# Two runs of four mixer chunks per batch instead of three runs, and the half tile moved to the last chunk

## The chip, the cores and the metric

The kernel runs on one core of a Trainium2 chip. TensorE (PE) multiplies matrices into PSUM banks, VectorE (DVE) and ScalarE (ACT) read those banks and work on SBUF, GpSimd (POOL) and SyncE (SP) issue DMAs. The metric is the device time of one launch in microseconds (us); smaller is better. Times quoted with a place, such as "358.13", are us from the first instruction of the profiled execution.

## The reference

Eight batches (B = 8) of a gated attention unit are followed by a low-rank token mixer. For each batch, with S = 3136 tokens, D = 256 channels and 64 query channels:

```
scores = (z @ z.T) / S            # S x S, z is S x 64
attn   = max(scores, 0) ** 2
x      = u * (attn @ v)           # S x 256, the attention's output
h      = (x.T @ U @ V).T          # U: S x 32, V: 32 x S
y      = x + h
out    = y + max(y @ w_ch1, 0) @ w_ch2     # 256 -> 1024 -> 256
```

The kernel multiplies in bf16 and accumulates in float32.

## The kernel before

**Tiles and turns.** The 3136 tokens are 24 tiles of 128 and one of 64 (tile 24, called NF in the code, the half tile). A batch is 25 *turns*; turn i makes the attention output of tile (12 + i) mod 25, so the half tile is turn 12. One turn is about 50 matmuls of line 471 (`half`), each with 64 contraction rows: two of them, on the upper and lower half of the array, run at the same time. The half tile's products (line 511, `quarter`) use quarters of the array, 64 by 64. Two turns share a pair of PSUM banks, of which there are two sets; `open_pair` takes the other set for each new pair of turns, and `close_pair` adds the two banks (ACT copy L485, DVE add L486), multiplies by u (L501) and leaves x in the SBUF pool `x_bf`. For the half tile two ACT copies (L497) and a DVE add (L498) stand between L486 and L501. The half tile is a pair of its own, turns 13 and 14 are the next pair.

**Scores.** `score` (L358) computes blocks of z zT two at a time into one of two PSUM buffers of the ring `ps2`; ACT applies max(.,0) (L371) and DVE squares (L373) into the panels A. Only half of the symmetric score matrix is computed; the other blocks come from DMA transposes of a panel into a *strip* (`turn`, L393, issued by SP). The strips are issued six turns ahead and there are seven strip buffers. Score steps of this batch stand in turns 0 to 9, those of the next batch in turns 14 to 24; turns 10 to 13 have none.

**The mixer of the batch before.** While batch b is attended, batch b-1 is mixed. After turn 0, `rank_sums` (L566) and `rank_close` (L578, L580) make t1 = x.T @ U. In seven of the turns `low_rank` (L621) computes V.T @ t1 for one *chunk* of three or four tiles into the PSUM set that is not being accumulated (`spare()`), two DVE instructions (L635) add it to x, and a DMA transpose (`turn_x`, L594) makes ut, the transposed chunk; there are three ut buffers. Where the next pair of turns begins, it opens that same set and waits for the two L635. A *burst* n is the four *up* steps of chunk n (L653: four matmuls each into a `ps2` buffer, then a relu on ACT, L671) merged with the *down* steps of chunk n-1 (L700: eight matmuls per tile into a bank of `spare()`, then a DVE add with x, L718, into one of two `o_sb` buffers, and a store, L731; the half tile needs a second DVE add, L726). Up and down use the whole 128 by 128 array; the half tile's down products use 128 by 64 halves of it. Burst 0 is special: every second up step goes to the spare set, with half the relu on DVE (L661).

Bursts stand together in *runs* behind a turn: `bursts_at` gives for each turn the bursts that follow it. In the kernel before, batch b runs bursts 6 and 7 of batch b-2 after turn 0, bursts 0 to 2 of batch b-1 after turn 6, and bursts 3 to 5 after turn 13. In the last batch, bursts 6 and 7 of batch 6 wait until attention is over (`late`), and batch 7 is mixed after that, burst by burst, with nothing beside it.

**What sets the order.** It is written out by hand: each engine takes its instructions in the order in which the Python code records them, and semaphores only make them wait. `place_groups` finds room in `x_bf` (34 tiles) from the turns at which chunks begin and end. `_merge` interleaves lists evenly, `_spread` puts score steps evenly between the 25 steps of a turn. `low_rank` is inserted into its turn at step 17, 12, 9 or 10.

The lines that matter below:

```
            if b and i in ahead:
                at = 17 if (i + (i > FIRST)) % 2 == 0 else 12 if i == 7 else 9 if i == 3 else 10
                main.insert(at, lambda c=ahead[i]: low_rank(b - 1, c))
...
            hold[0] = spare()[1 - n]          # down: bank 1 for the chunk's first pair of tiles, bank 0 for the second
```

Of the kernel before, what the change touches and what calls it, by code (L numbers as in the profile page):

```python
# [31 lines left out]
def _merge(*lists):  # L32

    keyed = [
        ((i + 0.5) / len(part), n, s)
        for n, part in enumerate(lists)
        for i, s in enumerate(part)
    ]
    return [s for _, _, s in sorted(keyed, key=lambda e: e[:2])]
# [3 lines left out]
def kernel(  # L43
# [100 lines left out]

    chunks = [[0, 1, 2, 3], [4, 5, 6, 7], [8, 9, 10, 11], [12, 13, 14]]
    chunks += [[15, 16, 17, 18], [19, 20, 21, 22], [23, 24]]
    chunks = [[turns(i) for i in c] for c in chunks]
    widths = [sum(P if t < NF else TAIL for t in c) for c in chunks]  # L150
    NC = len(chunks)
# [1 line left out]

    def bursts_at(b):

        at = {0: (NC - 1, NC)} if b > 1 else {}
        if b:
            at.update({6: (0, 1, 2), 13: (3, 4, 5)})
        if b == B - 1:
            at[17] = (NC - 1, NC)  # L160
        return at

    def place_groups():

# [512 lines left out]
    def down_steps(b, c):  # L677
        pairs = []
        for t in chunks[c]:
            if pair_of(t)[0] == t:  # L680
                pairs.append([])
            pairs[-1].append(t)
        at = {}
        for t in chunks[c]:
            at[t] = sum(P if k < NF else TAIL for k in at)
        hold = {}

        apart = b == B - 1 and c == NC - 1

        def step(n, k):  # L690
            pair = pairs[n]
            if k == 0:
                hold[0] = spare()[1 - n]
            ps = spare()[n] if apart and k else hold[0]
            q = at[pair[k]]
            for ht in range(NH):

                two = pair[k] == NF
                r = halves[ht % 2] if two else slice(0, P)
                mm(  # L700
                    out=ps[r, k * D : (k + 1) * D],
                    lhsT=relus[c][:, ht, q : q + (TAIL if two else P)],
                    rhs=w2_bf[:, ht, :],
                    start=(ht < 1 + two),
                    stop=(ht >= NH - 1 - two),
                )
            if apart or k == len(pair) - 1:
                k0 = k if apart else 0
                t, nk = pair[k0], k + 1 - k0
                if k0 == 0:  # L710
                    if c in (0, 3) and b + 2 < B:
                        hold[1] = both_pool.tile([P, 512], FP32, name="both")
                        hold[1] = hold[1].rearrange("p (t d) -> p t d", d=D)
                    else:
                        hold[1] = out_pool.tile([P, 2, D], FP32, name="o_sb")
                o_sb = hold[1][:, k0 : k + 1, :]
                p = P if t < NF else TAIL
                nc.vector.tensor_tensor(  # L718
                    out=o_sb[:p].rearrange("p t (a c) -> p t a c", c=P),
                    in0=split(ps[:p, k0 * D : (k + 1) * D]),  # L720
                    in1=x_at(b, t, nk)[:p],
                    op=ALU.add,
                )
                if t == NF:
                    o_flat = o_sb[:TAIL, 0, :]
                    nc.vector.tensor_tensor(  # L726
                        out=o_flat, in0=ps[halves[1], :D], in1=o_flat, op=ALU.add
                    )
                store = pool_dma if b + 1 < B else nc.sync.dma_start
                if t < NF:  # L730
                    store(out=rows(out[b])[:, t : t + nk, :], in_=o_sb)  # L731
                else:
                    store(out=out[b, NF * P :, :], in_=o_sb[:TAIL, 0, :])

        return [
            lambda n=n, k=k: step(n, k) for n in range(len(pairs)) for k in range(len(pairs[n]))
        ]
# [205 lines left out]
    for b in range(B):  # L943
        more = b + 1 < B
        begin = 0 if b else 2 * NG
        all_bursts.append(bursts_of(b))
        burst_at = bursts_at(b)
        v_in = list(V_PARTS) if more and b else []
        own = own_at if b else first_at
        wide = list(range(V_PARTS[3][0], NF, 2))  # L950
        wide = [(t, min(t + 2, NF)) for t in wide]
        fetch_at = dict(zip((12, 13, 14, 16, 17, 18, 20, 21), wide))
        cast_at = {i + 2: [] for i in fetch_at}
        ahead = dict(zip((2, 3, 4, 7, 10, 11, 14), range(NC)))
        for i in range(begin, NT):
            o = turns(i)
            fill = [s for key in own.get(i, ()) for s in score_steps(b, *key)]
            if b == 0 and i in first_new:
                fill += rebuild_steps(b, first_new[i])
            if b == 0 and i in first_more:  # L960
                fill.append(lambda args=first_more[i]: make_stored(*args))
            if b == 0 and i == begin:
                fill = panel + fill
            if more:
                coming = next_at if b else after_first
                fill += [s for key in coming[i] for s in score_steps(b + 1, *key)]
                if b and i == (1 if b > 1 else 5):
                    load_z(b + 1, WHOLE)
                if i == (7 if b > 1 else 11 - 2 * b):
                    turn_z(b + 1, (FIRST, NF))  # L970
                if i == (10 if b else 12):
                    turn_z(b + 1, (0, FIRST))
                if b == 0 and i == 14:
                    mirror_z((FIRST, NF))
                if i in (16, 18, 20) and v_in:
                    load_v(b + 1, v_in.pop(0))
                if b == 0 and i == 10:
                    load_v(b + 1, V_PARTS[-1])
                if b == 0 and i in cast_at:
                    (ta, tb), v_f = cast_at[i]  # L980
                    nc.gpsimd.tensor_copy(out=v_both[1][:, ta:tb, :], in_=v_f)
                if b == 0 and i == 15:
                    mirror_z((0, FIRST))
                    extend_z(b + 1)
            main = attend_steps(b, o)
            if b and i in ahead:
                at = 17 if (i + (i > FIRST)) % 2 == 0 else 12 if i == 7 else 9 if i == 3 else 10
                main.insert(at, lambda c=ahead[i]: low_rank(b - 1, c))
            _spread(main, fill)
            if b == 0 and i in first_turns:  # L990
                for t in first_turns[i]:
                    turn(b, t)
            else:
                now = b * NT + i
                for k in range(turned_to[0] + 1, min(now + lead(b, i), NT * B - 1) + 1):
                    turn(k // NT, turns(k % NT))
                    turned_to[0] = k
            if b == 0 and more and i in fetch_at:
                ta, tb = fetch_at[i]
                v_f = out_pool.tile([P, 2, D], FP32, name="o_sb")[:, : tb - ta, :]  # L1000
                nc.sync.dma_start(out=v_f, in_=rows(v[b + 1])[:, ta:tb, :])
                cast_at[i + 2] = (ta, tb), v_f
            if not more and i == NT - AHEAD:
                turn_x(b, 0)
            if b * NT + i in puts:
                puts[b * NT + i]()
            if (b, i) == ((1, 1) if more or b else (0, 20)):
                second_w()
            if b and i == 0:
                ps = spare()[0]  # L1010
                rank_sums(b - 1, ps)
                rank_close(b - 1, ps)
            for n in burst_at.get(i, ()):
                up, down = all_bursts[b - 1 if i else b - 2][n]
                if i and not more and n >= NC - 1:
                    late += up + down
                    up, down = [], []

                steps = [down.pop(0)] if n == 4 and n == burst_at[i][0] else []
                steps += _merge(up, down)  # L1020
                if more:
                    steps = _merge(steps, [lambda part=part: load_v(b + 1, part) for part in [v_in.pop(0)]])
                    if n == 3:
                        steps.insert(2, lambda: mirror_z((FIRST, NF)))
                        steps.insert(4, lambda: mirror_z((0, FIRST)))
                        steps.insert(6, lambda: extend_z(b + 1))
                run(steps)


# [49 lines left out]
```

## Time and profile before

| | |
|---|---|
| median of 3 runs | 992.9 us (992.23, 992.9, 1012.01) |
| the profiled execution's own time | 992.78 us |
| its span, first to last instruction | 991.1 us |
| TensorE busy | 981.4 us (99%) |
| ScalarE busy | 615.2 us (62%) |
| VectorE busy | 554.9 us (56%) |
| DMA transposes of strips, issue to landing, median | 5.4 us |
| stores from `o_sb` by POOL, issue to landing, median | 3.0 us |

Busy shares are averages over the whole span. Within a batch, a run begins after turn 6 at 363.81 and ends at 381.40, the half tile's turn begins at 396.54, the run behind turn 13 goes from 400.91 to 419.59. In these views, an instruction row gives its start, its duration (for a merged row, from the first start to the last end), engine, line, operation, operands and shapes, and how often it stands there; a matmul's duration contains its way through the array, so consecutive matmuls overlap, and what a matmul costs is read from start to start. The profiled program has the same lines as the kernel shown.

### The profile page before, as it was taken

How to read it: one execution, taken by the hardware profiler on the slowest of the kernel's cores; microseconds unless marked ns; L12 is line 12 of the kernel's file. 1: busy time of each engine (PE TensorE's matmuls, PEld its weight loads, DVE VectorE, ACT ScalarE, POOL GpSimd, SP SyncE). 2: the span in 40 equal slices, each digit the busy share in tenths (PEclk: the TensorE clock that was granted, in tenths of full speed). 3: DMA queues.
4: the chain of work that ended last, by engine and by line, in shares of the span. 5: the costliest groups of instructions: out<-in, count | busy, mean ns of one | idle time of the engine just before them, and what ended most of it. 6: DMA issues, size and time to landing. Idle time of an engine off the chain costs nothing.

```text
span 991.1 us, 31081 instructions
## 1 busy us (share of the span) xinstructions
PE 981.4 (99%) x13672; PEld 815.1 (82%) x13672; DVE 554.9 (56%) x1025; ACT 615.2 (62%) x845; POOL 172.9 (17%) x319
## 2 busy tenths in 40 slices
PE   8999999999999999999999999999999999999998
PEld 6788878888888888788887888878888788788876
DVE  6889834657446574375653655646546466352342
ACT  7978764757547575575745757467664676643154
POOL 5122112211121211212112121121211201111000
PEclk9999999999999999999999999999999999999999
DMA  9999979899799897898997999999889796595443
GB/s 189 167 200 229 203 155 215 149 193 184 148 177 183 165 181 144 182 180 172 169 162 168 190 162 171 164 169 187 156 166 193 156 189 135 117 201 115 81 109 100
DMA packets 400409, 165.40 MB, mean 167 GB/s; under 512 B 375617, under 2 KB 384001, under 8 KB 400273
## 3 DMA queue, kind: packets, MB, share of 16 engines
q1 hardware_dynamic: 372672, 98.11, 60.7%
q0 software_dynamic: 27600, 65.30, 27.1%
q8 instruction: 107, 1.75, 0.7%
q14 instruction: 30, 0.24, 0.1%
HBM read 61.88 MB, written 25.69 MB: 88 GB/s over the span
## 4 chain that ended last, share of the span: by engine, by line
PE 94%; DVE 3%; ACT 1%; DMA 1%; issue 0%; DVEq 0%
PE ps L471 49%; PE ps L653 17%; PE ps L700 17%; PE ps L358 7%; DVE A L373 2%; PE ps L621 1%; PE ps L511 1%; ACT A L371 1%; PE ps L566 1%; DMA strip<-A 1%; DVE both L486 0%; DMA out_dram<-o_sb 0%; PE ps L268 0%; DVE V_bf L331 0%; PE ps L284 0%
## 5 line engine op out<-in xcount | busy, mean ns | idle before, releaser
L371 ACT ACTIVATE A<-ps 128x832 bf16<-128x832 f32 (+9 forms) x481 | 358.0, 765 | 137.8 <-PE ps L358 132.5
L471 PE MATMUL ps<-v,A 64*128 64x256 bf16 x4988 | 341.2, 269 | 1.7 <-DVE A L373 1.6
L373 DVE TENSOR_TENSOR A<-A 128x832 bf16<-128x832 bf16 (+9 forms) x481 | 244.8, 527 | 130.4 <-ACT A L371 128.1
L471 PE MATMUL ps<-v,strip 64*128 64x256 bf16 x4420 | 310.1, 269 | 0.2 <-DMA strip<-A 0.2
L471 PEld LDWEIGHTS <-A 64*128 64x128 bf16 x4988 | 252.4, 94 | 40.7 <-issue 6.3
L671 ACT ACTIVATE relu_bf<-ps 128x1024 bf16<-128x1024 f32 (+2 forms) x208 | 188.2, 909 | 150.4 <-PE ps L653 150.4
L471 PEld LDWEIGHTS <-strip 64*128 64x128 bf16 x4420 | 227.6, 94 | 31.2 <-DMA strip<-A 0.8
L653 PE MATMUL ps<-ut,w_bf 128*128 128x512 bf16 (+2 forms) x896 | 201.5, 355 | 0.0
L700 PE MATMUL ps<-w_bf,relu_bf 128*128 128x256 bf16 (+1 forms) x1600 | 201.4, 273 | 0.0
L700 PEld LDWEIGHTS <-relu_bf 128*128 128x128 bf16 (+1 forms) x1600 | 152.9, 98 | 40.3 <-issue 4.9
L718 DVE TENSOR_TENSOR o_sb<-ps,x_bf 128x512 f32<-128x512 f32 (+2 forms) x81 | 54.8, 678 | 171.2 <-PE ps L700 167.3
L653 PEld LDWEIGHTS <-w_bf 128*128 128x128 bf16 x896 | 117.9, 144 | 37.4 <-issue 6.7
L358 PE MATMUL ps<-zT 64*128 64x416 bf16 (+8 forms) x812 | 134.8, 312 | 0.0
L455 POOL DMA_DIRECT2D u_sb<-in_u_dram x96 | 53.1, 553 | 423.2 <-DVE x_bf L501 411.3
L485 ACT COPY both<-ps 128x512 f32<-128x512 f32 (+1 forms) x104 | 59.0, 568 | 70.1 <-PE ps L471 64.0
L486 DVE TENSOR_TENSOR both<-ps,both 128x512 f32<-128x512 f32 (+1 forms) x104 | 69.2, 666 | 30.2 <-ACT both L485 29.7
L501 DVE TENSOR_TENSOR x_bf<-both,u_sb 128x512 bf16<-128x512 f32 (+1 forms) x104 | 69.8, 672 | 3.6
L635 DVE TENSOR_TENSOR x_bf<-ps,x_bf 128x512 bf16<-128x512 f32 (+1 forms) x112 | 65.5, 626 | 11.3 <-PE ps L621 11.2
L731 POOL DMA_DIRECT2D out_dram<-o_sb x66 | 36.0, 546 | 191.1 <-DVE o_sb L718 172.5
L358 PEld LDWEIGHTS <-zT 64*128 64x128 bf16 x812 | 46.3, 94 | 3.7
L718 DVE TENSOR_TENSOR both<-ps,x_bf 128x512 f32<-128x512 f32 (+1 forms) x24 | 15.0, 623 | 57.3 <-PE ps L700 57.3
L305 POOL DMA_DIRECT2D v<-in_v_dram x56 | 30.9, 553 | 2.4 <-DMA z_c<-in_z_dram 1.1
(65 smaller groups left out, 250.3 us busy)
## 6 DMA issues: line engine op xcount, KB each, us to landing
u_sb<-in_u_dram POOLq DMA_DIRECT2D x96, 256.0 KB, 4.3
out_dram<-o_sb POOLq DMA_DIRECT2D x66, 256.0 KB, 3.0
v<-in_v_dram POOLq DMA_DIRECT2D x52, 192.0 KB, 4.1
out_dram<-both POOLq DMA_DIRECT2D x18, 256.0 KB, 2.3
strip<-A SPq DMA_TRANSPOSE x194, 5.4
out_dram<-o_sb SPq DMA_DIRECT2D x11, 256.0 KB, 2.1
z_c<-in_z_dram POOLq DMA_DIRECT2D x7, 384.0 KB, 6.8
o_sb<-in_v_dram SPq DMA_DIRECT2D x7, 256.0 KB, 4.2
```

Of the source, the lines that this page charges most:

```text
L358: mm(out=ps[:, k, :n], lhsT=zT[halves[k], j + at[k], :], rhs=zT_flat[halves[k], c + at[k] * P : c + at[k] * P + n], start=True, stop=True,)
L371: nc.scalar.activation(out=dst, in_=src, func=AF.Relu, scale=sc)
L373: nc.vector.tensor_tensor(out=dst, in0=dst, in1=dst, op=ALU.mult)
L471: mm(out=acc[t0][h][:, (o - t0) * D : (o - t0 + 1) * D], lhsT=w[halves[h]], rhs=v_both[b % 2][halves[h], j, :], start=start, stop=stop, **kw,)
L485: nc.scalar.copy(out=both[:, :w], in_=banks[1][:, :w])
L486: nc.vector.tensor_tensor(out=both[:, :w], in0=banks[0][:, :w], in1=both[:, :w], op=ALU.add)
L501: nc.vector.tensor_tensor(out=x_at(b, t0, n), in0=split(both[:, :w]), in1=u_sb[:, :n, :].rearrange("p t (a c) -> p t a c", c=P), op=ALU.mult,)
L635: nc.vector.tensor_tensor(out=q, in0=split(ps[h][:, : len(ks) * D]), in1=q, op=ALU.add)
L653: mm(out=ps[i][:, :w] if apart else ps[:, i, :w], lhsT=w1_at[:, db, hp + i, :], rhs=uT[c][:, db, len(chunks[c]) * P - w :], start=(db == 0 ...
L671: nc.scalar.activation(out=relus[c][:, hp : hp + 2, :w], in_=ps[:, :, :w], func=AF.Relu)
L700: mm(out=ps[r, k * D : (k + 1) * D], lhsT=relus[c][:, ht, q : q + (TAIL if two else P)], rhs=w2_bf[:, ht, :], start=(ht < 1 + two), stop=( ...
L718: nc.vector.tensor_tensor(out=o_sb[:p].rearrange("p t (a c) -> p t a c", c=P), in0=split(ps[:p, k0 * D : (k + 1) * D]), in1=x_at(b, t, nk) ...
```

## The change

It touches four things.

1. The half tile (turn 12) leaves chunk 3 and becomes the first tile of chunk 6. Chunk 3 has two tiles instead of three, chunk 6 three instead of two.
2. There are two runs per batch in place of three: bursts 0 to 3 after turn 6, and bursts 4 to 7 after turn 12, the half tile's turn. In the last batch, bursts 4 and 5 of batch 6 follow turn 12, and 6 and 7 stay at the end.
3. `low_rank` of chunks 3 to 6 goes to turns 5, 7, 10 and 11 (before: 7, 10, 11, 14). Chunk 3's transpose is not issued there but after the up steps of burst 0.
4. In `down_steps` of the last chunk the half tile goes behind the chunk's two whole tiles, except in the last batch. The loads of v that stood in runs stand four in each run; the three copies that complete the next batch's zT stand in bursts 4 and 5 instead of burst 3.

```
-    chunks = [[0, 1, 2, 3], [4, 5, 6, 7], [8, 9, 10, 11], [12, 13, 14]]
-    chunks += [[15, 16, 17, 18], [19, 20, 21, 22], [23, 24]]
+    chunks = [[0, 1, 2, 3], [4, 5, 6, 7], [8, 9, 10, 11], [13, 14]]
+    chunks += [[15, 16, 17, 18], [19, 20, 21, 22], [12, 23, 24]]
...
-        at = {0: (NC - 1, NC)} if b > 1 else {}
-        if b:
-            at.update({6: (0, 1, 2), 13: (3, 4, 5)})
-        if b == B - 1:
-            at[17] = (NC - 1, NC)
-        return at
+        if not b:
+            return {}
+        if b < B - 1:
+            return {6: (0, 1, 2, 3), 12: (4, 5, 6, 7)}
+        return {6: (0, 1, 2, 3), 12: (4, 5), 17: (6, 7)}
...
             pairs[-1].append(t)
+        if b < B - 1:
+            pairs.sort(key=lambda pair: pair[0] == NF)
...
-        ahead = dict(zip((2, 3, 4, 7, 10, 11, 14), range(NC)))
+        ahead = dict(zip((2, 3, 4, 5, 7, 10, 11), range(NC)))
...
-                if i in (16, 18, 20) and v_in:
+                if i == 16 and v_in:
...
-                main.insert(at, lambda c=ahead[i]: low_rank(b - 1, c))
+                main.insert(at, lambda c=ahead[i]: low_rank(b - 1, c, None, c != 3))
...
-                up, down = all_bursts[b - 1 if i else b - 2][n]
-                if i and not more and n >= NC - 1:
+                up, down = all_bursts[b - 1][n]
+                if not more and n >= NC - 1:
                     late += up + down
                     up, down = [], []
-
-                steps = [down.pop(0)] if n == 4 and n == burst_at[i][0] else []
-                steps += _merge(up, down)
+                steps = _merge(up, down)
+                if n == 0:
+                    steps.append(lambda: turn_x(b - 1, 3))
                 if more:
                     steps = _merge(steps, [lambda part=part: load_v(b + 1, part) for part in [v_in.pop(0)]])
-                    if n == 3:
-                        steps.insert(2, lambda: mirror_z((FIRST, NF)))
-                        steps.insert(4, lambda: mirror_z((0, FIRST)))
-                        steps.insert(6, lambda: extend_z(b + 1))
+                    if n == 4:
+                        steps.insert(4, lambda: mirror_z((FIRST, NF)))
+                    if n == 5:
+                        steps.insert(2, lambda: mirror_z((0, FIRST)))
+                        steps.insert(4, lambda: extend_z(b + 1))
```

## The prediction

> **What bounds the kernel now.** I read the page first, then the timeline of one batch in the middle (turn 0 to turn 0 takes 120.9 us in each).
>
> ```profile
> PE 981.4 (99%) x13672; PEld 815.1 (82%) x13672; DVE 554.9 (56%) x1025; ACT 615.2 (62%) x845; POOL 172.9 (17%) x319
> ...
> PE 94%; DVE 3%; ACT 1%; DMA 1%; issue 0%; DVEq 0%
> ```
>
> TensorE holds the end: 99% busy, 94% of the chain that ended last. Nothing can be gained or lost but what TensorE does more, does less, or waits. So the sum has two columns: the cost of changing the array's tiling, which the change saves, and new waits of TensorE.
>
> **Saved: changes of tiling.** The TensorE timeline around the run behind turn 13 shows what a change costs.
>
> ```profile
> 400.71 0.27 PE L471 MATMUL ps<-v,A 64*128 64x256 bf16 x2
> 400.91 0.76 PE L653 MATMUL ps<-ut,w_bf 128*128 128x320 bf16 x4
> ...
> 401.51 1.04 PE L700 MATMUL ps<-w_bf,relu_bf 128*128 128x256 bf16 x8
> ...
> 402.39 0.71 PE L653 MATMUL ps<-ut,w_bf 128*128 128x320 bf16 x4
> ...
> 402.93 1.04 PE L700 MATMUL ps<-w_bf,relu_bf 128*128 128x256 bf16 x8
> ...
> 418.62 1.04 PE L700 MATMUL ps<-w_bf,relu_bf 128*128 128x256 bf16 x8
> ...
> 419.59 0.50 PE L471 MATMUL ps<-v,A 64*128 64x256 bf16 x6
> ```
>
> In the stream a pair of L471 takes 0.107 us; this last pair takes 0.20 (400.71 to 400.91). The first four L653 take 0.60 (to 401.51), the next four 0.54. Entering the whole array costs 0.09 + 0.06 = 0.15 us. Eight L700 take 0.87 in the stream and 0.97 before L471 (418.62 to 419.59): entering the half-row tiling costs 0.10, 0.01 more on the matmuls behind. In the order of the built instructions TensorE changes its tiling 106 times before and 88 times after: 11 fewer entries into the whole array, 7 fewer into half rows (the run after turn 0 is gone; the run behind the half tile is entered from its quarters; the half tile's products leave the middle of a run for its end). The matmuls are the same 13672. Saved: 11 x 0.15 + 7 x 0.11 = **2.4 us**.
>
> The Trainium skill, TensorEngine Tiling (Array Packing), Key Properties, states that a change of tiling mode drains TensorE, and TensorE: Matmul & The Clock Gate, Part 2, puts a drain at some 128 cycles, 0.053 us at 2.4 GHz. By that figure, an estimate, 18 changes would save 1.0 us; the rows are twice as dear, and the sum goes by them.
>
> **Added in each of seven batches (1 to 7).**
>
> *Start of the second run.* It now follows the half tile's close_pair at once.
>
> ```profile
> 398.08 1.48 PE L471 MATMUL ps<-v,A 64*128 64x256 bf16 x24
> 398.10 0.37 ACT L485 COPY both<-ps 128x256 f32<-128x256 f32 x1 [0.86 <-PE ps L511]
> ...
> 399.06 0.82 ACT L497 COPY both<-both 64x256 f32<-64x256 f32 x2 [0.59 <-DVE both L486]
> ```
>
> These ACT copies run beside turn 13 today. After the change the first up step starts at 398.08, is done at 399.0, and its relu (1.02 us for 512 columns) stands behind the L497 copies: 399.88 to 400.90 instead of 399.26 on. TensorE does one down tile (0.87) and the second up step (0.86), reaches the third at 400.74, and that needs the first's `ps2` buffer: 0.2 us of waiting. Bounds: 0 (relu first) and 0.6 (nothing beside it). I take 0.2; x 7 = **1.4 us**.
>
> *Turn 5.* Chunk 3's low_rank comes one turn after chunk 2's, into the same PSUM set.
>
> ```profile
> 356.16 0.44 PE L621 MATMUL ps<-t_sb,V_bf 64*128 64x256 bf16 x4
> ...
> 357.75 1.28 DVE L635 TENSOR_TENSOR x_bf<-ps,x_bf 128x512 bf16<-128x512 f32 x2
> 357.95 0.40 PE L358 MATMUL ps<-zT 64*128 64x416 bf16 x2
> 358.13 1.10 PE L471 MATMUL ps<-v,A 64*128 64x256 bf16 x16
> ```
>
> The new L621 stand after ten of these 16 L471, at 358.13 + 5 x 0.107 = 358.66. The second one writes the bank that the second L635 reads until 359.03: 0.4 us. DVE is behind here (L635 starts 1.2 us after its matmuls), so this is no accident of one batch. Bounds: 0.1 (what the same sequence costs at turns 2 and 3 today) and 0.6. I take 0.4; x 7 = **2.9 us**. Turn 6 opens that set 2.4 us later, when the new L635 (2 x 0.42, from 359.9) are done: nothing. Queued behind the waiting matmul is all of TensorE; DVE's and ACT's work shifts with it.
>
> *Turn 7.* It gets a chunk of four tiles where three stood.
>
> ```profile
> 383.54 1.02 DVE L635 TENSOR_TENSOR x_bf<-ps,x_bf 128x512 bf16<-128x512 f32 x2
> ...
> 384.60 0.71 PE L471 MATMUL ps<-v,A 64*128 64x256 bf16 x10
> ```
>
> Turn 8 opens the set at 384.60, just after the second L635 (ends 384.56; TensorE is held some 0.1 already). Two full adds take 1.28 instead of 1.02, so turn 8 opens 0.25 later. TensorE's own part is equal (three L621 occupy two slots, four do too). Bounds 0 and 0.36; x 7 = **1.8 us**.
>
> **At nothing.** Turn 11's low_rank loses a tile; its adds ended 0.1 before turn 12, now earlier. Chunk 3's transpose, SP-issued after burst 0, has two bursts (14 us) before its use; a ut lands in 3.7 (median). Chunks 5 and 6 keep the turns 10 and 11 of today's 4 and 5, so their ut land 158 to 164 in batch 1 against a half tile ending at 156.3: burst 5 starts 5 us later, burst 6 twelve; if that cover went, the wait would be a ut's lateness. The zT copies (2.0 us of DVE) lie between up steps as now. The loads of v start six turns later, but the last part goes at turn 16 as before, nine turns ahead of its use; each holds POOL 0.55 us, and what queues behind are stores. At the end of a second run the half tile's L718 waits for an `o_sb`, that is for a store issued 1.5 us before; DVE is held some 2 us into turn 13, where it has no work. Strips keep six turns of lead, 18 us against 5.4 to land; in the 19 turns that now follow each other without a run, SP needs 2.4 to 2.7 per strip when it issues them back to back (three in 8.06 us from 360.60) against 3.1 per turn. If that cover went, matmuls would wait for strips.
>
> **At the end, once.** (a) Attention over, batch 6's chunk 6 comes last, now with the half tile behind it, and batch 7's first up steps follow.
>
> ```profile
> 941.07 0.68 DVE L718 TENSOR_TENSOR o_sb<-ps,x_bf 128x512 f32<-128x512 f32 x1
> ...
> 942.04 0.55 POOL L731 DMA_DIRECT2D out_dram<-o_sb  x1 [2.38 <-DVE o_sb L718]
> 942.07 1.89 PE L653 MATMUL ps<-ut,w_bf 128*128 128x512 bf16 x8
> ```
>
> The half tile's add needs the buffer of the store issued at 942.04, median 3.0 to land: 945.1, then L718 and L726 (0.43 each), 946.1. TensorE has its matmuls (0.6) and an up step (0.9) until 943.7; the next step writes the half tile's bank. Wait: **2.4 us** (stores took 1.7 to 8.5: 1 to 8). (b) Batch 7's last chunk has three tiles in three groups and two `o_sb`: its last pair waits for the store before. From the end of chunk 5's products: add 0.9, store 2.1 (SP's median), two adds 0.8, so 3.8 against 2.5 today to the end of the last add; the half tile's products, now behind that point, bring it forward by 0.7: **0.6 us** (0 to 2).
>
> **Sum**, against the profiled execution's 992.78 (span 991.1; the median shown is 992.9, so no correction): -2.4 + 1.4 + 2.9 + 1.8 + 2.4 + 0.6 = +6.7, **999.5 us**. With every added cost at its lower bound (0, 0.7, 0, 1 and 0) it is 992.1, at the upper ones (4.2, 4.2, 2.5, 8 and 2) 1011.3.
>
> **Rivals.** *The waits don't bite*: TensorE reaches turn 5, turn 8 and the run as DVE and ACT come free, and only tilings count: 990.4. For it: DVE is but 56% busy; against it: the fences above. 17%. *DVE becomes the bound of turns 2 to 6*: from 348.0 to 363.8 it is busy 14.3 of 15.8 us, and turn 5 gives it 0.84 more; should that queue up to the relus of burst 0 instead of going into its gaps, 7 x 0.85 more: 1005.5. Against it: TensorE's own 0.4 + 0.1 us there widen the stretch. 12%. *Stores hold DVE*, the slow side: at six second runs DVE waits for a store with nothing to do until turn 14. That cover ends where a store takes over 5.5 us; the median is 3.0, the longest 8.5. If all six took 8.5, 6 x 3 us: 1017.5, slower by more than 2%. 4%. A tail store that slow would also cross the idle window of some 3.4 us behind which, by the Trainium skill (TensorE: Matmul & The Clock Gate, Part 1), the clock falls to half; the first seven matmuls here, 3.17 us where four later ones start 0.22 apart, show such a clock, and the granted one is 1.00 afterwards. That the edit does nothing is excluded by the instruction order.
>
> **The numbers.** My forecast (996 to 1003) has 64%, the rivals 17, 12 and 4, something unseen 3. 8 in 10 is 991.0 to 1004.5: all of the forecast, and most of the first two rivals' nearer side. Two per cent, about what a measurement of this kernel tells from no change, is 20 us: faster 1%, within 94%, slower 5%.
>
> **What would show it.** A batch of 121.4 us instead of 120.9; L621 in turn 5 with its second matmul 0.4 behind the first; L635 ending 0.25 later before turn 8; the third up step behind the half tile 0.2 late; a hole of 2.4 us in TensorE near 948. The forecast is wrong if the batch is shorter than 120.9, or if a strip or ut is what a matmul waits for.

## The result, and the profile after

The changed kernel takes 1000.87 us (median of 22 executions, 999.31 at the lowest) against 994.15 us (median of 22, 991.74 at the lowest): a ratio of **1.0075, 95% interval 1.0053 to 1.0097**, so it is 0.75% slower: the interval leaves out 1, and the difference is under 2%. The profiled execution took 999.82 us, with a span of 998.1 us. The forecast was 999.5 us. Some executions of every kernel here ran with a granted clock below 1.00 for a part of their time, which moves a median by several us, so below I compare ratios and, above all, the length of a batch at a clock of 1.00.

The page of the changed kernel: instructions of TensorE and the others, the chain that ended last, and the group of up matmuls (busy time, mean ns | idle time ahead of it and what ended most of that).

```profile
PE 980.5 (98%) x13632; PEld 823.7 (83%) x13672; DVE 556.4 (56%) x1025; ACT 614.3 (62%) x845; POOL 172.9 (17%) x319
...
PE 83%; issue 6%; DVE 4%; ACT 3%; DMA 2%; POOL 1%; DVEq 0%; POOLq 0%; ACTq 0%
...
L652 PE MATMUL ps<-ut,w_bf 128*128 128x512 bf16 (+2 forms) x856 | 197.4, 353 | 4.5 <-DVE o_sb L727 2.3
```

TensorE still holds the end. But its share of the chain falls from 94% to 83%, and those of the others grow: DVE's from 3% to 4%, ACT's from 1% to 3%, DMA's from 1% to 2%, "issue" from 0% to 6%, which is what waits look like from the end. (40 of the 896 up matmuls have no record here, so a part of "issue" can be only that gap; weight loads are complete at 13672.) The last number is the one long hole: 2.3 us before an up matmul, ended by DVE's L727, the half tile's last add. Line numbers up to the up steps are one lower than before (L471 is now L470, L621 L620, L635 L634, L653 L652), those of the down steps one higher (L718 is L719).

Busy time by stretches, first before, then after, cut at the same point of each batch, where ACT begins to wait for the first sum's copy. The columns are start:end, length, and busy us of PE, PEld, DVE, ACT and POOL, then granted clock, DMA share and GB/s.

```profile
225.66:346.58 120.92, 120.92 (x1707) 101.28 (x1703) 66.91 (x123) 75.58 (x103) 21.77 (x41) 1.00 0.94 171
...
830.24:991.10 160.86, 157.35 (x1886) 128.13 (x1880) 68.19 (x116) 75.40 (x97) 13.67 (x26) 1.00 0.56 122
```

```profile
225.43:347.97 122.54, 121.02 (x1702) 102.23 (x1703) 67.28 (x123) 75.46 (x103) 21.79 (x40) 1.00 0.98 169
347.97:469.29 121.32, 120.83 (x1702) 102.42 (x1703) 67.22 (x123) 75.45 (x103) 21.80 (x40) 1.00 0.95 170
...
833.26:998.10 164.84, 157.48 (x1876) 129.08 (x1880) 68.09 (x116) 75.25 (x97) 13.52 (x25) 1.00 0.57 119
```

A batch takes 121.32 us instead of 120.92, **0.40 more**, in every batch but one: batch 2 has 1.2 more than that, of which below. Before the cut of batch 1 (104.11 against 104.72) 0.6 us is won; the last stretch is 3.98 longer. So 7.0 us of span = 6 x 0.40 + 1.2 - 0.6 + 4.0.

The places that the prediction named, and first the hole of batch 2, on the timeline of the changed kernel (start, duration, engine, line; in brackets the idle time ahead and what ended it):

```profile
316.32 0.60 PE L470 MATMUL ps<-v,A 64*128 64x256 bf16 x8
...
317.95 0.28 PE L470 MATMUL ps<-v,A 64*128 64x256 bf16 x2 [1.04 <-issue]
...
480.59 1.28 DVE L634 TENSOR_TENSOR x_bf<-ps,x_bf 128x512 bf16<-128x512 f32 x2
...
481.51 0.68 PE L620 MATMUL ps<-t_sb,V_bf 64*128 64x256 bf16 x2
...
512.01 1.28 DVE L634 TENSOR_TENSOR x_bf<-ps,x_bf 128x512 bf16<-128x512 f32 x2
...
513.07 0.98 PE L470 MATMUL ps<-v,A 64*128 64x256 bf16 x10
...
527.71 0.82 ACT L496 COPY both<-both 64x256 f32<-64x256 f32 x2 [0.59 <-DVE both L485]
...
528.52 2.13 PE L652 MATMUL ps<-ut,w_bf 128*128 128x512 bf16 x8
528.55 3.22 ACT L670 ACTIVATE relu_bf<-ps 128x1024 bf16<-128x1024 f32 x3
...
530.49 1.04 PE L701 MATMUL ps<-w_bf,relu_bf 128*128 128x256 bf16 x8
...
946.07 0.54 POOL L732 DMA_DIRECT2D out_dram<-o_sb  x1 [0.67 <-DVE o_sb L719]
...
948.00 0.42 DVE L719 TENSOR_TENSOR o_sb<-ps,x_bf 64x256 f32<-64x256 f32 x1 [2.22 <-DMA out_dram<-o_sb]
948.45 0.42 DVE L727 TENSOR_TENSOR o_sb<-ps,o_sb 64x256 f32<-64x256 f32 x1
948.93 1.02 PE L652 MATMUL ps<-ut,w_bf 128*128 128x512 bf16 x4 [2.31 <-DVE o_sb L727]
```

Turn 5: the pair of L620 lasts 0.68 from the first start to the last end, where two that follow each other freely last 0.29; the second starts at 481.92, as chunk 2's second add ends (480.59 + 1.28 = 481.87). Turn 8: its opening waits at 513.35, for adds that end at 513.29. Start of the second run: the relu starts at 528.55, when ACT's copies are through (527.71 + 0.82), 0.90 us after the down matmuls behind its own started (527.65); the two up steps ahead of 530.49 take 1.97 us from start to start, where eight such matmuls take 1.73. Tail: DVE is idle 2.22 us until a store has landed, and TensorE, behind it, 2.31.

From start to start of all matmuls of a steady batch, less what their columns take, the whole difference can be read:

| us per batch | before | after | predicted difference | measured |
|---|---|---|---|---|
| changes of tiling (11, then 8) with what follows on the second matmul | 1.30 | 0.89 | -0.40 | -0.41 |
| start of the second run | 0 | 0.24 | +0.2 | +0.24 |
| turn 5, second L620 | - | 0.39 | +0.4 | +0.39 |
| turn 8, opening | 0.11 | 0.27 | +0.25 | +0.17 |
| turn 7, half of the rows idle beside an odd L621 | 0.11 | 0 | 0 | -0.11 |
| turns 3 and 4: L620 twice, opening | 0.30 | 0.41 | 0 | +0.12 |
| first run, first down step | 0.10 | 0.04 | 0 | -0.06 |
| sum | | | +0.45 | +0.34 (0.40 by the batch's length) |

### The profile page after: what moved, and what is told of

The parts are those of the page before. It is cut to its first block, busy times and chain, and to the rows that moved or that the text cites. A ratio compares the mean times of both kernels' runs of the same rounds, so it can differ in the third digit from the quotient of the medians.

```text
span 998.1 us, 31002 instructions
## 1 busy us (share of the span) xinstructions
PE 980.5 (98%) x13632; PEld 823.7 (83%) x13672; DVE 556.4 (56%) x1025; ACT 614.3 (62%) x845; POOL 172.9 (17%) x319
## 4 chain that ended last, share of the span: by engine, by line
PE 83%; issue 6%; DVE 4%; ACT 3%; DMA 2%; POOL 1%; DVEq 0%; POOLq 0%; ACTq 0%
PE ps L470 44%; PE ps L701 16%; PE ps L652 15%; PE ps L357 6%; ACT A L370 2%; DVE both L485 1%; DMA strip<-A 1%; DVE A L372 1%; PE ps L620 1%; DVE x_bf L634 1%; DVE x_bf L500 1%; ACT relu_bf L670 1%; PE ps L565 1%; ACT both L484 1%; DMA out_dram<-o_sb 1%
## 5 line engine op out<-in xcount | busy, mean ns | idle before, releaser
L470 PE MATMUL ps<-v,A 64*128 64x256 bf16 x4988 | 344.0, 270 | 2.3 <-DVE A L372 1.1
L372 DVE TENSOR_TENSOR A<-A 128x832 bf16<-128x832 bf16 (+9 forms) x481 | 243.9, 525 | 138.1 <-ACT A L370 136.4
L470 PE MATMUL ps<-v,strip 64*128 64x256 bf16 x4420 | 312.1, 269 | 0.6 <-DMA strip<-A 0.4
L470 PEld LDWEIGHTS <-A 64*128 64x128 bf16 x4988 | 258.5, 94 | 40.0 <-issue 11.0
L470 PEld LDWEIGHTS <-strip 64*128 64x128 bf16 x4420 | 232.7, 94 | 28.2 <-DMA strip<-A 1.5
L652 PE MATMUL ps<-ut,w_bf 128*128 128x512 bf16 (+2 forms) x856 | 197.4, 353 | 4.5 <-DVE o_sb L727 2.3
L701 PE MATMUL ps<-w_bf,relu_bf 128*128 128x256 bf16 (+1 forms) x1600 | 200.9, 273 | 0.6 <-DVE o_sb L719 0.2
L701 PEld LDWEIGHTS <-relu_bf 128*128 128x128 bf16 (+1 forms) x1600 | 152.9, 98 | 38.8 <-issue 3.6
L719 DVE TENSOR_TENSOR o_sb<-ps,x_bf 128x512 f32<-128x512 f32 (+2 forms) x87 | 57.3, 660 | 178.0 <-PE ps L701 161.3
L652 PEld LDWEIGHTS <-w_bf 128*128 128x128 bf16 x896 | 118.8, 144 | 40.3 <-issue 8.9
L357 PE MATMUL ps<-zT 64*128 64x416 bf16 (+8 forms) x812 | 137.7, 312 | 0.0
L485 DVE TENSOR_TENSOR both<-ps,both 128x512 f32<-128x512 f32 (+1 forms) x104 | 69.4, 667 | 34.3 <-ACT both L484 33.4
L634 DVE TENSOR_TENSOR x_bf<-ps,x_bf 128x512 bf16<-128x512 f32 (+1 forms) x112 | 65.5, 627 | 11.2 <-PE ps L620 11.1
L357 PEld LDWEIGHTS <-zT 64*128 64x128 bf16 x812 | 49.3, 94 | 3.2
L719 DVE TENSOR_TENSOR both<-ps,x_bf 128x512 f32<-128x512 f32 x18 | 12.4, 692 | 44.0 <-PE ps L701 44.0
```

The costliest lines, as they stand in the source:

```text
L357: mm(out=ps[:, k, :n], lhsT=zT[halves[k], j + at[k], :], rhs=zT_flat[halves[k], c + at[k] * P : c + at[k] * P + n], start=True, stop=True,)
L372: nc.vector.tensor_tensor(out=dst, in0=dst, in1=dst, op=ALU.mult)
L470: mm(out=acc[t0][h][:, (o - t0) * D : (o - t0 + 1) * D], lhsT=w[halves[h]], rhs=v_both[b % 2][halves[h], j, :], start=start, stop=stop, **kw,)
L485: nc.vector.tensor_tensor(out=both[:, :w], in0=banks[0][:, :w], in1=both[:, :w], op=ALU.add)
L634: nc.vector.tensor_tensor(out=q, in0=split(ps[h][:, : len(ks) * D]), in1=q, op=ALU.add)
L652: mm(out=ps[i][:, :w] if apart else ps[:, i, :w], lhsT=w1_at[:, db, hp + i, :], rhs=uT[c][:, db, len(chunks[c]) * P - w :], start=(db == 0 ...
```

## The experiments

Most edits are of one kind: one suspected wait of the changed kernel is taken away, and the batch is measured again. They are compared with its 121.32 us per batch and its last stretch of 164.84 us. One edit adds a run, to measure a price by itself.

### Turn 5 alone

```
-        ahead = dict(zip((2, 3, 4, 5, 7, 10, 11), range(NC)))
+        ahead = dict(zip((2, 3, 4, 6, 7, 10, 11), range(NC)))
```

> The changed kernel with chunk 3's low_rank in turn 6 instead of turn 5; nothing else differs, the same matmuls and the same adds. **My theory** (the second L620 of turn 5 waits only for the bank that chunk 2's second add still reads, 0.39 us in each of seven batches; in turn 6 the other PSUM set is free): that wait goes and none takes its place, so a batch takes 120.9 us instead of the 121.32 measured in the changed kernel, and the time falls by 2.8 us. **Rival, DVE bounds turns 2 to 6**: its adds are the same ones one turn later and still stand ahead of burst 0, so the wait only moves (to the opening of turn 6 or to burst 0's relus), the batch stays within 0.1 us of 121.32 and the time within 0.7 us.

Measured: a batch of 120.93 us (0.39 less) in four of the six; batch 2 took 121.04 and batch 6 121.49, of which below. Lowest time 996.62, ratio to the kernel before 1.0054 (1.0009 to 1.0098). Its timeline in turn 6:

```profile
482.79 0.68 DVE L485 TENSOR_TENSOR both<-ps,both 128x512 f32<-128x512 f32 x1
...
483.59 0.29 PE L620 MATMUL ps<-t_sb,V_bf 64*128 64x256 bf16 x2
...
484.71 2.17 PE L652 MATMUL ps<-ut,w_bf 128*128 128x512 bf16 x9
...
485.05 0.75 DVE L634 TENSOR_TENSOR x_bf<-ps,x_bf 128x256 bf16<-128x256 f32 x2
```

The pair of L620 lasts 0.29 and follows the sum that frees its bank (L485 ends 483.47). The adds, the same two, now run beside the first up steps of the run, and hold nothing. So 0.39 us was the wait for a bank, and the rival, that DVE bounds this stretch, is out: DVE does the same work there and the batch is shorter by the whole wait.

### Start of the second run: another order

```
-                steps = _merge(up, down)
+                steps = [down.pop(0)] if n == 4 else []
+                steps += _merge(up, down)
```

> The changed kernel with the second run opened by one of chunk 3's down steps ahead of the first up step, as the run behind turn 13 was before. **My theory** (the first relu queues behind ACT's copies of the half tile, and the third up step waits 0.24 us for its buffer): the down step puts 0.87 us of TensorE work ahead of the first up step, ACT is through with its copies by then, the wait goes, and a batch takes 121.08 instead of 121.32: 1.7 us in seven batches. **Rival**: the order of up and down steps is not what delays it (the relus are slower than the steps that they feed), the wait moves to the next up step and the batch stays at 121.3. **Second rival**: the down step's bank is one that the half tile's sum is still read from, so TensorE waits some 0.6 to 0.8 us at the start of the run instead, and a batch takes 121.7 to 121.9.

Measured: 121.93 us in four batches, 0.61 more, and 122.14 in batch 2, of which below; ratio to the kernel before 1.0094 (1.0045 to 1.0144). My theory gave the wrong sign. The second rival was right about the batch and the bank, though only a part of the time is lost at that bank.

```profile
541.27 1.03 PE L701 MATMUL ps<-w_bf,relu_bf 128*128 128x256 bf16 x8 [0.38 <-ACT both L484]
...
546.94 1.02 PE L652 MATMUL ps<-ut,w_bf 128*128 128x512 bf16 x4 [0.31 <-ACT relu_bf L670]
```

The down step writes a bank that ACT still copies for the half tile's sum, and TensorE waits for it: 0.65 us pass from the last product of the half tile to the first L701, 0.45 more than to the first L652 in the changed kernel. And with two down steps at the beginning and none between later ones, two up steps meet at the relus again (0.48). Less the 0.24 that is gone, and 0.06 on the second matmul that is not paid here, this is the 0.61. The order in which a run starts is a trade between the two.

### Start of the second run: the copies off ACT

```
-                nc.scalar.copy(out=both[halves[r], w : 2 * w], in_=both[halves[1 - r], :w])
+                nc.vector.tensor_copy(out=both[halves[r], w : 2 * w], in_=both[halves[1 - r], :w])
```

> The changed kernel with the half tile's two cross copies (both<-both, 64x256, before on ACT) on DVE. **My theory** (the second run's third up step waits 0.24 us because the first relu queues behind these copies on ACT): the relu starts as its matmuls end, the wait goes, and a batch takes 121.08 instead of 121.32; 1.7 us in all. **Rival** (the third up step waits because two up steps follow each other and a relu of 1.02 us is slower than an up step of 0.86): 0.1 to 0.24 us of the wait stays and a batch takes 121.2 to 121.3. DVE has some 0.8 us more to do there, at a place where it has no other work until the first group's products are summed.

Measured: 121.09 us in all six batches, 0.24 less; lowest time 996.72, ratio to the kernel before 1.0053 (1.0013 to 1.0093).

```profile
525.17 1.08 PE L652 MATMUL ps<-ut,w_bf 128*128 128x512 bf16 x4
...
526.16 0.59 DVE L496 COPY both<-both 64x256 f32<-64x256 f32 x2
526.35 1.02 ACT L670 ACTIVATE relu_bf<-ps 128x1024 bf16<-128x1024 f32 x1 [0.79 <-PE ps L652]
...
526.97 1.89 PE L652 MATMUL ps<-ut,w_bf 128*128 128x512 bf16 x8
...
528.69 1.04 PE L701 MATMUL ps<-w_bf,relu_bf 128*128 128x256 bf16 x8
```

The relu starts 0.26 us after the down matmuls that follow its own (526.35, 526.09) where it was 0.90 (528.55, 527.65), and the two up steps take 1.72 us. So the cause was the queue on ACT, and not the length of a relu. On DVE both copies take 0.59 us, on ACT 0.82.

### The hole at the end: the order of the products

```
-        if b < B - 1:
+        if b < B - 2:
             pairs.sort(key=lambda pair: pair[0] == NF)
```

> The changed kernel with the half tile's products first in batch 6's chunk 6, as before the change; batches 0 to 5 keep them last. **My theory** (the hole of 2.3 us near 947 is the half tile's add waiting for the store that holds its buffer, and the bank that it reads is what batch 7's second up step writes): the hole goes, two more changes of tiling come back (0.25 us), and the time falls by 2.1 us, all of it behind turn 24 of the last batch; the batches stay at 121.32. **Rival**: the store's buffer is short at any order, the pairs' adds wait in place of the half tile's, and the time falls by less than 0.5 us.

Measured: a last stretch of 164.79 us, 0.05 less; the batches stay at 121.32. The rival was right.

```profile
948.55 1.91 PE L701 MATMUL ps<-w_bf,relu_bf 128*128 128x256 bf16 x16 [0.76 <-DVE o_sb L719]
...
952.04 0.69 DVE L719 TENSOR_TENSOR o_sb<-ps,x_bf 128x512 f32<-128x512 f32 x1 [2.76 <-DMA out_dram<-o_sb]
952.79 1.02 PE L652 MATMUL ps<-ut,w_bf 128*128 128x512 bf16 x4 [1.47 <-DVE o_sb L719]
```

The same 2.2 us in two pieces, and now it is a whole pair's add (128x512) that waits 2.76 us for the store. The place in the order is not what costs; it is that the chunk has one more group to store than before.

### The hole at the end: a third buffer

```
-                    if c in (0, 3) and b + 2 < B:
+                    if (c in (0, 3) and b + 2 < B) or (c == NC - 1 and b + 2 >= B and t == NF):
                         hold[1] = both_pool.tile([P, 512], FP32, name="both")
```

> The changed kernel with the half tile's sum of chunk 6 in the last two batches taken from a `both` buffer (idle by then) instead of `o_sb`; the order of the products stays as the change has it. The run with the other order kept 2.5 us of waiting in that place, so the order is not what costs. **My theory now** (chunk 6 has three stored groups since it took in the half tile, `o_sb` has two buffers, so the last add waits for a store, whichever group it is): with a third buffer the hole of 2.3 us near 947 goes, and the last add of all no longer waits 1.7 us of DVE time for a store: 2.3 + 0.8 = 3.1 us less, all behind the last batch's attention; the batches stay at 121.32. **Rival** (batch 7's first up steps find no free bank there in any case, since TensorE outruns DVE's adds): the hole shrinks to 1 us or so and what is left is put down to DVE's add; 1.5 us less.

Measured: a last stretch of 161.55 us, 3.29 less; lowest time 994.80, ratio to the kernel before 1.0031 (1.0003 to 1.0058).

```profile
946.41 2.10 PE L652 MATMUL ps<-ut,w_bf 128*128 128x512 bf16 x8
946.57 0.41 DVE L719 TENSOR_TENSOR both<-ps,x_bf 64x256 f32<-64x256 f32 x1
946.95 0.54 POOL L732 DMA_DIRECT2D out_dram<-o_sb  x1 [0.67 <-DVE o_sb L719]
947.01 0.43 DVE L727 TENSOR_TENSOR both<-ps,both 64x256 f32<-64x256 f32 x1
```

The half tile's add goes at once, and the eight up matmuls take 2.04 us from start to start of what follows, where they took 4.35. That is 2.31; the rest, 0.98, is at the very end, where the last add no longer waits for a store (from the start of the last sixteen down matmuls to the end of the span 5.0 instead of 6.0).

### The price of a change of tiling

```
-            return {6: (0, 1, 2, 3), 12: (4, 5, 6, 7)}
-        return {6: (0, 1, 2, 3), 12: (4, 5), 17: (6, 7)}
+            return {6: (0, 1, 2), 8: (3,), 12: (4, 5, 6, 7)}
+        return {6: (0, 1, 2), 8: (3,), 12: (4, 5), 17: (6, 7)}
```

> The changed kernel with burst 3 taken out of the first run and put behind turn 8 as a run of its own: the same matmuls, one more entry into the whole array and one more exit into half rows in each of seven batches. **My theory** (0.09 + 0.06 on entering, 0.10 on leaving): 0.25 us per batch, so 121.57 instead of 121.32, and 1.75 us in all, provided that no wait comes or goes at the new place, which the trace will show separately. **By the Trainium skill** (TensorE: Matmul & The Clock Gate, Part 2: a drain is some 128 cycles, 0.053 us at 2.4 GHz, an estimate) two changes would cost 0.11 us per batch, 0.75 us in all. **Rival, changes of tiling cost nothing by themselves**: 121.32.

Measured: 121.67 us in every batch, 0.345 more; ratio to the kernel before 1.0087 (1.0052 to 1.0123). The added run:

```profile
510.99 0.66 PE L652 MATMUL ps<-ut,w_bf 128*128 128x256 bf16 x4
511.48 1.04 PE L701 MATMUL ps<-w_bf,relu_bf 128*128 128x256 bf16 x8
512.36 0.60 PE L652 MATMUL ps<-ut,w_bf 128*128 128x256 bf16 x4
...
515.41 1.04 PE L701 MATMUL ps<-w_bf,relu_bf 128*128 128x256 bf16 x8
516.38 0.72 PE L470 MATMUL ps<-v,A 64*128 64x256 bf16 x10
```

The first four L652 take 0.49 (to 511.48), the next four 0.43 (the eight L701 behind those start at 512.79): the 0.06 on the second matmul. The last eight L701 take 0.97 where others take 0.88: leaving costs 0.098. Entering costs 0.095 ahead of 510.99. Together 0.25, as predicted. What is over, 0.09, is no later wait: against the kernel with the copies on DVE, whose turns are the same up to there, one half of the array's rows is 0.26 and the other 0.35 late from the end of the added run to the half tile's turn, without a change in between. There the second of two L470 starts 0.02 behind the first, here 0.003; why, stays open. The estimate from the Trainium skill's drain (TensorE: Matmul & The Clock Gate, Part 2) is 0.11 for the two changes, less than half of the measured 0.25.

### All three together, and beyond

The first kernel has chunk 3 in turn 6, the copies on DVE and the third buffer. The next two add other places for `low_rank` to it:

```
-                at = 17 if (i + (i > FIRST)) % 2 == 0 else 12 if i == 7 else 9 if i == 3 else 10
+                at = {4: 19, 7: 8}.get(i, 17 if (i + (i > FIRST)) % 2 == 0 else 9 if i == 3 else 10)
...
+                at = {2: 15, 4: 19, 7: 8}.get(i, 17 if (i + (i > FIRST)) % 2 == 0 else 9 if i == 3 else 10)
```

> The changed kernel with three mends together: chunk 3's low_rank in turn 6, the half tile's copies on DVE, and the third buffer for chunk 6 in the last two batches. **If the costs are separate waits**, they add: a batch of 121.32 - 0.39 - 0.24 = 120.7, and 7 x 0.63 + 3.1 = 7.5 us less than the changed kernel, of whose span 998.1 some 1.2 us was a hole of one batch: a span of 989.5 to 990.6, against 991.1 before, so faster than both by a little (0.1 to 0.2%). **Rival, one resource behind them all** (DVE late in turns 2 to 6, or the relus in the runs): the waits move from one place to the next, the batch stays above 120.92, and it is no faster than before.

Measured: 120.70 us in the four undisturbed batches and a last stretch of 160.92: the waits add up, to within 0.01 us, and no common resource stands behind them. In time it can't be told from the kernel before: lowest 990.69 against 991.04, ratio 1.0021 (0.9984 to 1.0058). The shortest span, 989.0, is a little under the 989.5 to 990.6 that were expected.

> The kernel with three mends (a batch of 120.70 where undisturbed) and two more: chunk 4's low_rank in turn 7 at step 8 instead of 12, and chunk 2's in turn 4 at step 19 instead of 17. What is left there are 0.27 us at the opening of turn 8 (the second L634 of chunk 4 still reads the bank) and 0.155 at chunk 2's first L620 (the pair's sum L485 still reads it). **If these are waits for a bank and nothing else**, both go: a batch of 120.27, 3.0 us in seven batches, a span near 986.6 where nothing disturbs, 0.45% under the kernel before. **Rival** (DVE has no room in turns 4 and 7, and the adds displace the evictions of A that its own matmuls need): the waits turn up at L470 and a batch stays at 120.6 or above.

Measured: 120.62 us in all batches but batch 2 (121.84, of which below), a span of 990.2; median 992.17 against 996.53 for the kernel before, lowest 989.75 against 991.32, ratio **0.9965 (0.993 to 1.0)**: a third of a per cent faster by the ratio, but the interval reaches no difference. The batch is where the rival put it. Of the two waits chunk 2's went (the batch gains 0.08 of its 0.155), the other stayed to the hundredth, 0.274. The timeline shows why; its first row is used at the end of this document, the others are turn 7:

```profile
316.83 0.28 PE L470 MATMUL ps<-v,A 64*128 64x256 bf16 x2 [1.05 <-issue]
...
508.49 0.76 ACT L370 ACTIVATE A<-ps 128x704 bf16<-128x704 f32 x1 [1.02 <-PE ps L357]
508.62 0.38 PE L620 MATMUL ps<-t_sb,V_bf 64*128 64x256 bf16 x4
...
509.28 0.52 DVE L372 TENSOR_TENSOR A<-A 128x704 bf16<-128x704 bf16 x1 [0.82 <-ACT A L370]
...
509.73 1.28 DVE L634 TENSOR_TENSOR x_bf<-ps,x_bf 128x512 bf16<-128x512 f32 x2
```

The matmuls are done 0.45 earlier after the run's end than they were, but the adds stand behind an eviction of A in DVE's queue (L372), which waits 0.82 us for ACT's first eviction after the run. The adds are bound by that, not by their matmuls.

> As the kernel with five mends, and chunk 0's low_rank in turn 2 at step 15 instead of 17. Left is the 0.26 us of chunk 1's second L620 in turn 3, which waits for chunk 0's second L634. **If the adds go ahead of the next eviction of A on DVE**, this wait goes too: a batch of 120.0, 1.8 us less than with five mends. **Rival** (DVE is full from turn 2 to turn 4, 0.6 us of eviction moved behind the adds is what TensorE then waits for, or the bank isn't free so early): the wait changes its place, and the batch is at 120.3 or above.

Measured: 120.62 us, no difference; ratio 0.9963 (0.9926 to 1.0). The 0.26 us at chunk 1's second L620 stays, and again DVE's order is the reason: the matmuls are 0.2 us earlier, but the adds still stand behind the same two evictions and start 3.85 us after the batch's cut in both kernels. The rival was right about the batch; the wait did not change its place.

## Why the prediction was right

**Saved tilings** (2.4 us): right. The 18 changes fall on the six batches with a run behind turn 0 before, 0.40 in each, and 0.41 was measured. The extra run shows the price, 0.25 for one entry and one exit, in a kernel where nothing else was to change.

**Start of the second run** (0.2 x 7): right in place, cause and size, 0.24; moving the copies off ACT takes away exactly that.

**Turn 5** (0.4 x 7): right, 0.39; moving chunk 3 takes it away. The rival about DVE falls with it.

**Turn 7** (0.25 x 7): the mechanism was right and the size too large. Turn 8 opens 0.28 us later after the run's end (3.48 instead of 3.20), as put, but 0.11 of that is the fourth L620 itself, which turn 11 has less; the wait grew by 0.17. The step "TensorE's own part is equal (three L621 occupy two slots, four do too)" overlooked that the half slot beside the third L621 was idle time of 0.106 that the change wins back. 1.8 us should have been some 0.4.

**Tail (a)** (2.4): the size was right, 2.31, and the buffer as the cause; the reading that the half tile's place "behind it" makes it was wrong. With the half tile first the wait is as long. What costs is three stored groups for two buffers, which the prediction had seen for (b) alone. **Tail (b)** (0.6): 0.98.

**At nothing**: two things were not nothing. Chunk 1's second L620, chunk 2's first and turn 4's opening together wait 0.12 us more per batch than before, 0.8 us in all. DVE's sum of the first pair ends 0.12 later there (2.21 instead of 2.08 after the cut). It is not that DVE has less time: the square ahead of this sum ends 1.48 after the cut, and ACT's copy for it 1.34, in both kernels. Why the sum starts 0.11 later stays open. The 0.6 us won at the start are a wait for an eviction by DVE at 96.9 in batch 0 (0.65 in all): the changed kernel hasn't it, four of its variants have it again near that place (0.4 to 2.8 us), so it can't be put down to the change. The other covers held: no up matmul waits for a ut and no L470 for a strip in a steady batch, and DVE is held 2 us into turn 13 (to 549.3, the run ends at 547.24) without anyone waiting.

**The rival of held stores** did occur once, in small: in the kernel with chunk 3 in turn 6, one second run has DVE waiting 3.59 us for a store and TensorE 0.49 behind it.

**The sum**: predicted +6.7, measured +7.0. Six batches gave 2.4 us and the last stretch, with the seventh batch in it, 4.0 (3.3 of it goes with the third buffer): 6.4, where the prediction had 3.7 for seven batches and 3.0 for the tail. 0.6 us was won at the start, and 1.2 us of the hole in batch 2 belongs to no step. That 999.5 and 999.82 are so close is thus in part luck: without those last two the span would be 0.3 us below the forecast. And within the steps errors cancel: the 1.4 us too much for turn 7 stand against 0.8 that were put at nothing, 0.4 too little at the very end and 0.3 too little at the start of the second run.

## What to carry to other kernels

Where one engine is busy 99% of the time, count the changes of its mode at their measured price, but then walk each moved instruction to the bank, buffer and queue that it meets at its new place: here waits of 0.2 to 2.3 us came to more than three times the saving. Moving an instruction a turn on, to another engine's queue or to an idle buffer gave three of them back in full. And before moving a producer earlier, look at what stands ahead of its consumer in the consumer's own queue.

## What was not expected of the hardware

**A hole in which nothing waits.** In batch 2 of the changed kernel TensorE stands still for 1.04 us, and its idle time is put down to "issue": no semaphore holds it (317.95 in the timeline above). The kernel with five mends has the same hole, 1.05 us, at the same matmuls (316.83), just ahead of a load of u, and the one with three mends has 1.32. Of the other seven variants, whose program is nearly the same, three lose 0.1 to 0.3 us there and four nothing. What goes with the hole is in the view of the transfers, GB/s in 40 slices; first the changed kernel from 316 to 318 us, then the one with only the copies on DVE from 314 to 317, the same place:

```profile
GB/s 5 0 5 26 41 31 41 31 41 31 41 36 41 5 10 10 10 5 10 10 10 10 10 10 5 15 10 123 292 292 297 282 297 276 297 287 297 282 292 287
```

```profile
GB/s 55 58 109 58 113 109 225 116 287 290 283 198 440 379 348 280 321 215 246 273 219 215 157 116 246 283 300 287 283 300 290 283 297 283 294 263 225 185 390 182
```

With the hole, the DMA engines move at most 41 GB/s until 317.35, for the last 0.7 us of it 15 or less, and then nearly 300; without it, never under 55. So transfers and TensorE's instructions stand still together.

The list of single DMA packets in the traces shows more. Queue q8, which the profile calls "instruction", moves 107 packets of 16 KB in an execution, one for some 256 of TensorE's 27344 matmuls and weight loads. From this count I take it that they bring TensorE's instructions; the profile does not say so. One such packet is the last to land before the weight load behind the hole (the same weight load in every kernel):

| kernel | packet lands | weight load starts later by | batch 2 longer by |
|---|---|---|---|
| three mends | 322.55 | 1.50 | 1.50 |
| changed kernel | 316.57 | 1.38 | 1.22 |
| five mends | 315.44 | 1.39 | 1.22 |
| third buffer | 317.44 | 1.37 | 0.30 |
| down step first | 329.99 | 1.46 | 0.21 |
| chunk 3 in turn 6 | 314.88 | 1.47 | 0.11 |
| extra run | 315.45 | 1.78 | 0 |
| order of the products | 319.96 | 1.86 | 0 |
| six mends | 321.35 | 3.18 | 0 |
| copies on DVE | 312.01 | 4.53 | 0 |
| before | 306.94 | 6.08 | 0 |

Where the packet lands early, nothing waits; in the six kernels where it lands late, TensorE goes on 1.37 to 1.50 us after the landing, and the batch is longer. So the hole is most likely a wait for instructions, which no semaphore shows. Some of these packets take long (2.34 us in the changed kernel, 2.97 with three mends, 1.03 in the median), others start late; why, and why the other transfers are slow at the same time, was not settled. It costs 0.1 to 1.5 us of a batch when it comes.
